# A Nystrom attention and two MLP layers on one core: how q and k are turned, when weights are narrowed, where block 2's weights are put

## The chip, the cores and the metric

One core of one Trainium2 chip runs the whole program in one launch. The metric is device time in microseconds (us); here the median of three runs of the kernel before. Engines are named as in the profile: PE (TensorE matmul), PEld (its weight loads), DVE (VectorE), ACT (ScalarE), POOL (GpSimd), SP (SyncE, which issues most DMAs).

## The reference

q, k, v are 4 batches x 8 heads x 576 rows x 64. Every 18 rows of q and k are averaged to 32 landmarks. Three softmaxes follow, A from q and the landmarks of k, B from both landmarks, C from the landmarks of q and k, and an iterated inverse of B:

```python
A, Bm, C = sm(q, k_lm), sm(q_lm, k_lm), sm(q_lm, k)
Z = Bm.T / (norm1(Bm) * norminf(Bm) + 1e-6)
for _ in range(6):
    Z = 2 * Z - Z @ Bm @ Z
x = (A @ Z @ C @ v)                          # 2304 tokens x 512
h = x @ w_in;  g = max(h, 0) + alpha * min(h, 0);  x = g @ w_out      # d_ff 2048
h = x @ w_in2; g = h * clip(h + 3, 0, 6) / 6;      out = g @ w_out2
```

The weights arrive as 64-bit floats and are narrowed to 32 bits on the core.

## The kernel before, in words

**Stages.** The attention of batch 0 runs alone at the start (`attention(0, ..., lat=0)`). Then the first MLP layer (block 1) runs over the four batches, each in two half batches of 288 tokens, and the attention of the next batch runs in between (`bg`, a background generator that is stepped by `tick`, three times per step). Last comes the second MLP layer (block 2) over five groups of 512 or 384 tokens.

**Steps.** A half batch has 16 steps, one for each 128 columns of the hidden layer (`NK` = 16). `items` is the list of all steps; `at_` is the step's number in its batch, 0 to 31 (L896). `Block1.first` (L741) forms h on PE and applies the activation on ACT and DVE. `Block1.second` (L767) multiplies by w_out into four accumulators `acc`, two steps later (`LOOK`, L733; three for the first one). Block 1 doesn't multiply x by w_in: `project` (L667) multiplies w_in by `bd`, the small product of the inverse, C and v of each head, so that A of the batch can be multiplied by the result. One call covers 512 columns, that is four steps, into two PSUM banks of a pool that has two (`two`, L226); its casts (`split`, L126) are ACT work and then DVE work, and free the banks.

**Narrowing.** A piece of 128 x 512 weights lands as pairs of 32-bit words (`landed`, L180). `words_of` (L189) is two ACT instructions on it (L196, L199), `joined` (L201) one DVE instruction (L206). `w_in_tiles` (L627) goes through w_in: the first 512 columns (block c = 0) as eight half pieces, the others as four pieces each; each of its steps issues the words of one piece and the join of the one before. Its loads of blocks 2 and 3 use the four buffers that block 0's pieces leave. `w_out_tiles` (L690) narrows one piece of w_out a step. The first half batch uses w_out in plain 32-bit; later ones use pairs of 32-bit parts made by `w_out_split` (L695).

**Order.** In `attention(0, ...)` all engines but POOL keep the order in which the code issues (`manual_schedule`, L708). In the main loop (L888) only PE and SP do; the order on ACT and DVE is set by a planner, by a modelled timeline and the order of issue. `behind(insts)` (L172) makes what it encloses follow the given instructions in the queue of the same engine; it adds no wait on another engine. In the first half batch, step `at_` issues narrowing up to a count, w_in up to piece `at_ + 12`, w_out up to `at_ + 3`, all behind `started`, the split of project(0,0)'s first 256 columns (L726). The second 256 columns and project(0,1) are issued at step 1. The last two query tiles of A (`rest`, L590) are in `bg` from step 0; batch 1's attention enters it at step 8 and is finished at step 28, ahead of project(1,0).

**The turns of q and k.** `transposed_long` (L282): a load has rows p x 4 + t on partition p. For each of the four head pairs eight matmuls with the identity (four t by two heads, each two instructions in the profile) write a PSUM bank in the order (t, p), ACT copies the bank to SBUF with a write of stride four words (L299), DVE sums over the landmarks (L300). `warm(n)` (L711) issues n matmuls on zeros to an idle bank.

**Block 2's weights.** 32 units (`units2`, L860), in the order `order2`: four tiles of w_in2, four of w_out2, for each of four chunks. Each is loaded to a place, narrowed and split there. `homes` lists the places: at first new ones and one spare, then those of block 1's projected w_in and of w_out, which come free as the last half batch uses them for the last time. Odd batches use the hidden columns in another order (`part`, L623): blocks 2, 3, 0, 1. `land2` issues loads, `upto2` narrowing, up to a count that grows with the step.

## Time and profile before

| what | value |
|---|---|
| median of 3 runs | 897.0 us (896.64 to 897.53) |
| profiled execution | 897.17 us, span 895.2 us |
| mean granted clock of TensorE | 0.979 |
| PE, PEld, DVE, ACT busy | 849.7, 726.8, 420.6, 381.7 us |
| L758 relu, 128 x 288, ACT | 410 ns each, x116 |
| L128 cast of gs, 128 x 288, ACT | 433 ns each, x112 |
| L206 join, 128 x 512, DVE | 691 ns each, x32 in block 2 |
| L430 scores of A, first half batch, PE wait ahead | 3.8 us |

The span runs from the first to the last instruction of the profiled execution; its own time is 2 us longer. A busy PE is not PE at its peak: `warm` matmuls count as busy. In the rows below a line begins with a start and a duration in us (timeline, chain of waits), or with the bounds of a stretch. In the timeline the duration reaches to the end of the last matmul of a group, so groups overlap by some 0.2 us; the chain of waits counts from one to the next. In brackets stands the time that the engine was idle before, and what released it. A clock of 1.00 is TensorE's full speed.

### The profile page before, as it was taken

The page shows a single profiled execution, that of the slowest core. Times are in us where ns is not written, and L with a number is a line of the kernel's source. Part 1 is how long each engine was busy: PE and PEld are TensorE (multiplying, and loading weights), DVE is VectorE, ACT ScalarE, POOL GpSimd, SP SyncE. Part 2 cuts the span into 40 slices and gives each one's busy share as a digit, 9 for nine tenths or more (in the row PEclk, how much of TensorE's full clock was granted, in tenths as well). Part 3 has the DMA queues.
Part 4 walks back from the last instruction along what each step waited for, and adds up shares of the span by engine and source line. Part 5 has one row for each costly group of instructions (what it writes and reads, how often), then busy time and mean ns, then how long its engine had stood idle before and what let it go on. Part 6 is the DMA issues. An engine that isn't in the chain of part 4 may idle for free.

```text
span 895.2 us, 13601 instructions
## 1 busy us (share of the span) xinstructions
PE 849.7 (95%) x5487; PEld 726.8 (81%) x5487; DVE 420.6 (47%) x880; ACT 381.7 (43%) x811; POOL 27.6 (3%) x51
## 2 busy tenths in 40 slices
PE   9856999999999999999999499999999999999997
PEld 4524779989999989988998388888888888989996
DVE  3677457755754557468447822232223222223222
ACT  4488245545434544358449922222222222222222
POOL 0000001010010101010100000000000000000000
PEclk9977999999999999999999799999999999999999
DMA  7986312351044311059227600210021002000000
GB/s 229 408 306 209 67 40 68 85 156 54 1 107 128 89 38 55 1 181 367 86 73 244 246 0 1 94 48 0 1 71 48 0 1 88 30 1 12 25 0 36
DMA packets 60847, 82.68 MB, mean 92 GB/s; under 512 B 35696, under 2 KB 43888, under 8 KB 59504
## 3 DMA queue, kind: packets, MB, share of 16 engines
q1 hardware_dynamic: 57648, 68.18, 24.0%
q0 software_dynamic: 3136, 13.63, 4.1%
q8 instruction: 43, 0.70, 0.3%
q14 instruction: 20, 0.16, 0.1%
HBM read 63.45 MB, written 18.35 MB: 91 GB/s over the span
## 4 chain that ended last, share of the span: by engine, by line
PE 82%; ACT 8%; DMA 5%; DVE 2%; issue 1%; SPq 1%; ACTq 0%; DVEq 0%
PE h L134 30%; PE oacc L134 22%; PE acc L134 17%; DMA raw<-in_moe_w_in_dram 3%; ACT raw L196 3%; ACT raw L199 3%; PE acc L776 3%; PE wp L676 2%; DMA raw<-in_moe_w_out_dram 2%; PE tp L271 1%; PE sa L430 1%; ACT w L128 1%; PE idle L713 1%; PE sc L343 1%; PE psr L514 1%
## 5 line engine op out<-in xcount | busy, mean ns | idle before, releaser
L134 PE MATMUL oacc<-w,g 128*128 128x512 f32 x864 | 211.5, 394 | 11.4 <-ACT g L128 11.4
L134 PE MATMUL acc<-gs,wout 128*128 128x288 f32 x1344 | 208.4, 300 | 4.4 <-DVE gs L129 2.4
L134 PE MATMUL h<-ysb,w 128*128 128x512 f32 (+1 forms) x960 | 210.5, 368 | 0.0
L134 PEld LDWEIGHTS oacc<-w,g 128*128 128x128 f32 x864 | 163.2, 190 | 44.7 <-ACT g L128 11.8
L134 PEld LDWEIGHTS h<-ysb,w 128*128 128x128 f32 x960 | 176.6, 188 | 25.0
L134 PEld LDWEIGHTS acc<-gs,wout 128*128 128x128 f32 x1344 | 185.2, 188 | 10.1 <-DVE gs L129 3.7
L807 DVE SCALAR_TENSOR_TENSOR t<-t,h 128x512 f32<-128x512 f32 (+1 forms) x80 | 50.8, 635 | 220.6 <-ACT t L806 220.6
L806 ACT ACTIVATE t<-h,three 128x512 f32<-128x512 f32 (+1 forms) x80 | 51.6, 645 | 218.9 <-PE h L134 218.7
L134 PE MATMUL h<-a,w 128*128 128x288 f32 x768 | 130.1, 306 | 3.1 <-DVE gs L755 2.6
L134 PEld LDWEIGHTS h<-a,w 128*128 128x128 f32 x768 | 109.8, 190 | 21.8 <-DVE gs L129 11.1
L758 ACT ACTIVATE t<-h 128x288 f32<-128x288 f32 x116 | 47.6, 410 | 70.4 <-PE h L134 69.7
L759 DVE SCALAR_TENSOR_TENSOR t<-t,beta,h 128x288 f32<-128x288 f32 x112 | 57.2, 511 | 43.2 <-ACT t L758 42.1
L129 DVE TENSOR_TENSOR g<-t,g 128x512 fp32r<-128x512 f32 (+1 forms) x80 | 51.1, 639 | 45.8 <-ACT g L128 45.5
L128 ACT CAST g<-t 128x512 fp32r<-128x512 f32 (+1 forms) x80 | 46.1, 578 | 51.2 <-DVE t L807 51.2
L128 ACT CAST gs<-t 128x288 fp32r<-128x288 f32 x112 | 48.5, 433 | 44.4 <-DVE t L759 44.1
L129 DVE TENSOR_TENSOR gs<-t,gs 128x288 fp32r<-128x288 f32 x112 | 50.9, 454 | 29.7 <-ACT gs L128 29.5
L196 ACT ACTIVATE raw<-raw 128x512 f32<-128x512 f32 (+1 forms) x68 | 44.6, 659 | 8.1 <-DMA raw<-in_moe_w_in_dram 6.1
L199 ACT ACTIVATE raw<-raw 128x512 int32<-128x512 uint32 (+1 forms) x68 | 43.8, 648 | 0.0
L776 PE MATMUL acc<-gs,raw 128*128 128x288 f32 x128 | 36.3, 421 | 0.0
L676 PE MATMUL wp<-win,bd 64*32 64x512 f32 (+1 forms) x272 | 21.4, 602 | 11.7 <-DVE w L129 9.5
L206 DVE SCALAR_TENSOR_TENSOR x<-raw 128x512 int32<-128x512 int32 x32 | 22.1, 691 | 15.2 <-ACT raw L199 14.9
L776 PEld LDWEIGHTS acc<-gs,raw 128*128 128x128 f32 x128 | 24.3, 202 | 5.6 <-issue 1.0
(170 smaller groups left out, 583.6 us busy)
## 6 DMA issues: line engine op xcount, KB each, us to landing
raw<-in_moe_w_in_dram SPq DMA_DIRECT2D x32, 512.0 KB, 7.2
raw<-in_moe_w_out_dram SPq DMA_DIRECT2D x32, 512.0 KB, 10.2
win<-w_in SPq DMA_DIRECT2D x6, 1024.0 KB, 4.8
ysb<-y_d SPq DMA_DIRECT2D x6, 1024.0 KB, 13.6
y_d<-ys POOLq DMA_DIRECT2D x16, 288.0 KB, 3.6
y_d<-a POOLq DMA_DIRECT2D x16, 288.0 KB, 4.0
out_dram<-ob SPq DMA_DIRECT2D x18, 256.0 KB, 2.0
rk<-in_k_dram SPq DMA_DIRECT2D x16, 256.0 KB, 4.8
```

What stands on the lines that cost most here:

```text
L128: nc.scalar.copy(hi, src),
L129: rest.tensor_tensor(out=lo, in0=src, in1=hi.bitcast(F32), op=ALU.subtract),
L134: nc.tensor.matmul(ps, lhsT=lhs(x), rhs=rhs(y), start=first and i == 0, stop=last and i == 2)
L196: nc.scalar.activation(out=high.bitcast(F32), in_=high.bitcast(F32), func=AF.Prelu, scale=2.0 ** -112, alpha=-(2.0 ** 32))
L199: nc.scalar.activation(out=low, in_=low.bitcast(U32), func=AF.Copy, scale=0.9374 * 2.0 ** -29)
L206: nc.vector.scalar_tensor_tensor(out=to.bitcast(I32), in0=high, scalar=3, in1=low, op0=ALU.logical_shift_left, op1=ALU.bitwise_or)
L676: nc.tensor.matmul(ps[g][js], lhsT=bd_t[b][gp, js], rhs=w[gp, j, cols], start=True, stop=True)
L758: nc.scalar.activation(out=t, in_=h, func=AF.Relu, scale=-1.0),
L759: nc.vector.scalar_tensor_tensor(out=gs[:, 0] if plain else t, in0=t, scalar=beta[:, kk:kk + 1], in1=h, op0=ALU.mult, op1=ALU.add),
L776: nc.tensor.matmul(acc, lhsT=words[kk][:, ms], rhs=gs[:, 0], start=at_ == 0, stop=at_ == NK - 1)
L806: nc.scalar.activation(out=t, in_=h, func=AF.Relu, bias=three, scale=1.0)
L807: nc.vector.scalar_tensor_tensor(out=t, in0=t, scalar=6.0, in1=h, op0=ALU.min, op1=ALU.mult)
```

## The change

- In `transposed_long` the matmuls write every fourth word of the bank (`t:FULL:NF`), so that it is in order, and ACT's copy is dense. The tails warm once instead of three times, the turns not at all.
- `norms` is no longer a generator. In batch 0's attention the groups' maxima and exponentials stand in a loop with blocks and norms after the first; the pieces of `a0`, `a1` are moved, warm counts are lower, and nine steps of `early` (w_in narrowing) are issued in place of five.
- project(0,0)'s second 256 columns are issued at step 0 and are `started`; project(0,1) to (0,3) come at steps 3, 7 and 11 instead of 1, 5 and 9. Narrowing in step `at_` is issued behind `started` for three steps and then behind steps `at_ - 2` and `at_ - 3`; w_out goes first, up to `at_ + 2`, w_in up to `at_ + 10`.
- In the first half batch even steps use DVE for the activation, odd ones ACT and DVE (before: DVE for the first 12).
- `rest` enters `bg` at step 6.
- Block 2 has ten new places instead of eight; the places of w_out are listed in the order in which the last batch uses w_out; the counts of `land2` and `upto2` follow.

```diff
--- before.py
+++ after.py
@@ -286,21 +286,20 @@
             for j in range(NP):
                 nc.tensor.transpose(ps[:, j, :TAIL], tail[:, NG * j:NG * j + NG, :], ident[:TAIL, :TAIL])
             nc.scalar.copy(xt[:, :, FULL:S], ps[:, :, :TAIL])
-            warm(3)
+            warm(1)
             yield True
             for j in range(NP):
-                ps = bank("tp").rearrange("q (t p) -> q t p", t=NF)
+                ps = bank("tp")
                 for t in range(NF):
                     for g in range(NG):
                         nc.tensor.matmul(
-                            ps[64 * g:64 * g + 64, t], lhsT=full[:, NG * j + g, t * D:(t + 1) * D], rhs=ident,
+                            ps[64 * g:64 * g + 64, t:FULL:NF], lhsT=full[:, NG * j + g, t * D:(t + 1) * D], rhs=ident,
                             start=True, stop=True,
                         )
-                nc.scalar.copy(xt[:, j, :FULL].rearrange("q (p t) -> q t p", t=NF), ps)
+                nc.scalar.copy(xt[:, j, :FULL], ps)
                 nc.vector.tensor_reduce(
                     out=lm[:, j], in_=xt[:, j, :S].rearrange("p (l r) -> p l r", r=W), op=ALU.add, axis=AX.X
                 )
-                warm(3)
                 yield True
 
         if not lat:
@@ -408,7 +407,6 @@
             nc.vector.tensor_scalar(out=cc, in0=cc, scalar1=1e-6, scalar2=None, op0=ALU.add)
             nc.vector.reciprocal(out=cc, in_=cc)
             nc.vector.tensor_scalar(out=cn, in0=cc, scalar1=-1.0, scalar2=None, op0=ALU.mult)
-            yield True
 
         def c_scale():
             nc.vector.tensor_tensor(out=rs[:, :, 0:1], in0=sm[:, :, 0:1], in1=sm[:, :, 2:3], op=ALU.add)
@@ -556,35 +554,31 @@
             most_b(range(NG))
             for g in range(NG):
                 exp_b(g)
-            most_c(0, 1)
-            most_c(0, 0)
-            bias_c(0)
-            blocks()
-            warm(6)
-            exp_c(0)
-            n_ = norms()
-            drain(n_)
-            most_c(1, 1)
-            most_c(1, 0)
-            bias_c(1)
-            exp_c(1)
+            for g in range(NG):
+                most_c(g, 1)
+                most_c(g, 0)
+                bias_c(g)
+                exp_c(g)
+                if g == 0:
+                    blocks()
+                    warm(4)
+                    norms()
+            drain(turned_c(0))
+            next(a0)
             c_scale()
+            next(a1)
+            drain(turned_c(1))
+            next(early)
             warm(4)
-            drain(turned_c(0))
-            next(a1)
-            next(a0)
-            warm(2)
-            drain(turned_c(1))
-            warm(2)
             drain(product())
             n0, n1 = normalised([0, 1]), normalised([2])
             next(early)
-            fill = [a0, early, a1, early, a1, n0, early, n0, n1, early, n1, turned([0, 1]), turned([2])]
-            for _ in inverse():
-                for _ in range(2):
+            fill = [early, a0, a1, early, early, a1, early, n0, early, n0, n1, early, n1, early, turned([0, 1]), turned([2])]
+            for i, _ in enumerate(inverse()):
+                for _ in range(3 if i < 3 else 2):
                     if fill:
                         next(fill.pop(0), None)
-                warm(5)
+                warm(4)
             for x in fill:
                 next(x, None)
             rest.append(in_order(scores([3]), scores([4]), normalised([3]), normalised([4]), turned([3]), turned([4])))
@@ -607,7 +601,8 @@
         for x in pieces:
             yield from scores(x)
             yield from wait(1)
-        yield from norms()
+        norms()
+        yield True
         yield from alternate(turned_c(0), turned_c(1))
         yield from wait(1)
         yield from product()
@@ -729,7 +724,7 @@
     ps_o = pool("ps_o", 4, space=PSUM)
     ps_h = pool("ps_h", 2, space=PSUM)
 
-    w2, ysb = {}, {}
+    w2, ysb, steps = {}, {}, []
     LOOK = 2
 
     class Block1:
@@ -748,11 +743,12 @@
             plain = self.b == self.blk == 0
             t = mm.tile([P, HS], F32, tag="t", name="t")
             gs = mm.tile([P, 2, HS], F32 if plain else F32R, tag="gs", name="gs", bufs=5)
-            if plain and at_ < 3 * NK // 4:
+            if plain and at_ % 2 == 0:
                 nc.vector.tensor_scalar(
                     out=t, in0=h, scalar1=0.0, scalar2=minus[:, kk:kk + 1], op0=ALU.min, op1=ALU.mult
                 )
-                nc.vector.tensor_tensor(out=gs[:, 0], in0=t, in1=h, op=ALU.add)
+                self.last = [nc.vector.tensor_tensor(out=gs[:, 0], in0=t, in1=h, op=ALU.add)]
+                steps.append(self.last)
                 return gs
             self.last = [
                 nc.scalar.activation(out=t, in_=h, func=AF.Relu, scale=-1.0),
@@ -760,6 +756,7 @@
                     out=gs[:, 0] if plain else t, in0=t, scalar=beta[:, kk:kk + 1], in1=h, op0=ALU.mult, op1=ALU.add
                 ),
             ]
+            steps.append(self.last)
             if not plain:
                 split(gs[:, 0], gs[:, 1], t)
             return gs
@@ -867,7 +864,7 @@
             yield True
 
     bg = Background()
-    emitted = [NP + 1, 0, 0]
+    emitted = [0, 2 * NP + 1, 0]
 
     def pinned(gen):
         while True:
@@ -876,7 +873,6 @@
                     return
             yield True
 
-    bg.add(pinned(rest[0]))
     g2, ring = [], [0]
     units = Background(units2())
     done2 = [0]
@@ -897,13 +893,13 @@
 
             if n < n1:
                 if b == 0 and at_ < NK:
-                    for i, (gen, upto) in enumerate(((w_gen, min(at_ + 12, NK + 5)), (wo_gen, min(at_ + 3, NK)))):
-                        with behind(started):
+                    if at_ == 0:
+                        started = project(0, 0, slice(256, 512))
+                    for i, (gen, upto) in enumerate(((wo_gen, min(at_ + 2, NK)), (w_gen, min(at_ + 10, NK + 5)))):
+                        with behind(started if at_ < 3 else steps[at_ - 2] + steps[at_ - 3]):
                             gen.step(upto - emitted[i])
                         emitted[i] = upto
-                    if at_ == 1:
-                        project(0, 0, slice(256, 512))
-                    if at_ % 4 == 1 and at_ // 4 + 1 < NC:
+                    if at_ % 4 == 3 and at_ // 4 + 1 < NC:
                         project(0, at_ // 4 + 1)
                 if b == 0 and at_ >= NK - 2:
                     upto = min(NK, at_ - NK + 3)
@@ -913,6 +909,8 @@
                 if b == 0 and at_ in (NK + 4, NK + 6):
                     c = NC // 2 + (at_ - NK - 4) // 2
                     nc.gpsimd.dma_start(out=keep[:, c], in_=wins[c])
+                if b == 0 and at_ == 6:
+                    bg.add(pinned(rest[0]))
                 if b == 0 and at_ == 8 or b and at_ == 5:
                     if b + 1 < B:
                         bg.add(rush(attention(b + 1, two, 1), 300))
@@ -927,17 +925,19 @@
                     stx.close()
                     wz = pool("wz", 1, side="right")
                     yp = pool("yp", 2, side="right")
-                    homes += [(wz, f"z{i}") for i in range(8)] + [(wa, f"s{NK - 1}")]
-                    free = [f"s{(i + NK) % (NK + 1)}" for i in range(NK)]
+                    nz = 10
+                    homes += [(wz, f"z{i}") for i in range(nz)] + [(wa, f"s{NK - 1}")]
+
+                    free = [f"s{(4 * part(b, i // 4) + i % 4 + NK) % (NK + 1)}" for i in range(NK)]
                     for i in range(NC):
                         homes += [(wc, f"c{2 * i}"), (wc, f"c{2 * i + 1}")] + [(wa, x_) for x_ in free[4 * i:4 * i + 4]]
-                    land2(9)
+                    land2(nz + 1)
                     load_y(0)
                     load_y(1)
                 if b == B - 1 and at_ > 4:
                     if at_ >= NK + 4:
-                        land2(min(len(order2), 9 + 6 * ((at_ - NK) // 4)))
-                    upto2(min(at_ - 4, 9) if at_ < NK + 4 else 9 + 5 * (at_ - NK - 3) // 4)
+                        land2(min(len(order2), nz + 1 + 6 * ((at_ - NK) // 4)))
+                    upto2(min(3 * (at_ - 3) // 4, nz + 1) if at_ < NK + 4 else nz + 1 + 5 * (at_ - NK - 3) // 4)
             if n == n1:
                 for _ in range(2):
                     pair = ay.tile([P, 2, 2, 512], F32R, tag="at", name="g2")
```

## Rows read from the trace of the kernel before

**Rows 1.** page, part 1: busy us of each engine, share of the span, instructions.
```profile
PE 849.7 (95%) x5487; PEld 726.8 (81%) x5487; DVE 420.6 (47%) x880; ACT 381.7 (43%) x811; POOL 27.6 (3%) x51
```

**Rows 2.** busy time by stretch: length, then busy us and count of each engine, clock, DMA, GB/s.
```profile
0.00:48.43 48.43, 44.37 (x405) 25.18 (x405) 23.38 (x73) 21.96 (x49) 1.52 (x9) 1.00 0.91 325
48.43:130.74 82.31, 62.81 (x381) 44.90 (x381) 51.58 (x104) 49.15 (x101) 2.87 (x6) 0.88 0.50 151
...
490.00:520.00 30.00, 18.63 (x70) 14.69 (x69) 21.52 (x34) 23.95 (x44) 2.63 (x4) 0.77 0.57 217
```

**Rows 3.** what PE waited for: us in total, times, longest us.
```profile
PE oacc L134 <- ACT g L128: 11.4, 1, 11.4
PE wp L676 <- DVE w L129: 9.5, 1, 9.5
```

**Rows 4.** chain of waits, the turns of k: start, us, what.
```profile
5.98 1.02 PE tp L295 x16
7.00 0.75 PE idle L713 x3
```

**Rows 5.** timeline of ACT, opening: start, us, what; behind it idle before and releaser.
```profile
20.64 1.08 ACT L299 COPY qT<-tp 128x512 f32<-128x512 f32 x1 [0.69 <-PE tp L295]
...
30.41 0.58 ACT L474 COPY ct<-ctp 128x512 f32<-128x512 f32 x1
...
41.77 0.21 ACT L530 COPY nx<-psr 128x64 f32<-128x64 f32 x1 [1.01 <-DVE nx L390]
```

**Rows 6.** timeline of DVE, opening.
```profile
21.75 0.75 DVE L300 TENSOR_REDUCE qlm<-qT 128x32 f32<-128x576 f32 x1 [1.01 <-ACT qT L299]
```

**Rows 7.** busy time by stretch, one us of the opening.
```profile
11.00:12.00 1.00, 1.00 (x16) 0.76 (x16) 0.27 (x1) 0.69 (x1) 0.00 (x0) 1.00 0.73 65
```

**Rows 8.** timeline of PE, first half batch.
```profile
48.43 0.79 PE L676 MATMUL wp<-win,bd 64*32 64x256 f32 x16
...
63.59 2.29 PE L676 MATMUL wp<-win,bd 64*32 64x512 f32 x16 [9.53 <-DVE w L129]
65.81 3.25 PE L134 MATMUL h<-a,w 128*128 128x288 f32 x12
...
77.51 5.35 PE L776 MATMUL acc<-gs,raw 128*128 128x288 f32 x16
```

**Rows 9.** chain of waits, first half batch.
```profile
93.72 1.94 PE acc L776 x8
95.66 0.80 PE h L134 x6
...
102.02 1.86 PE wp L676 x16
```

**Rows 10.** timeline of ACT, first half batch.
```profile
49.30 0.65 ACT L128 CAST w<-wp 128x256 fp32r<-128x256 f32 x2 [1.46 <-PE wp L676]
...
52.92 0.65 ACT L196 ACTIVATE raw<-raw 128x512 f32<-128x512 f32 x1
...
54.05 0.65 ACT L196 ACTIVATE raw<-raw 128x512 f32<-128x512 f32 x1
...
62.29 0.62 ACT L128 CAST w<-wp 128x256 fp32r<-128x256 f32 x2
```

**Rows 11.** chain of waits, start of block 2.
```profile
505.29 0.66 ACT raw L196
...
506.91 0.67 ACT raw L196
...
510.82 5.49 PE oacc L134 x12
...
519.41 2.72 PE oacc L134 x12
```

**Rows 12.** timeline of PE, second half batch: end of the next batch's attention.
```profile
169.35 0.44 PE L537 MATMUL psv<-r,vd 128*64 128x128 f32 x4
...
173.91 1.09 PE L676 MATMUL wp<-win,bd 64*32 64x512 f32 x16
```

## The prediction

> **What bounds the kernel now.** I read the page's part 1 first: TensorE (PE) is busy 95% of the span [rows 1], so only the stretches in which it stands still, or works for nothing, can be shortened. The busy times by stretch find them [rows 2]. Opening, 0 to 48.43 us: PE looks busy (44.37), but `warm` matmuls are part of that; the chain of waits shows each turn of a head pair as 1.02 us of transposes and 0.75 of warm, one after the other [rows 4]. First half batch, 48.43 to 130.74: PE stands 82.31 - 62.81 = 19.5 us, at a mean clock of 0.88 instead of 1.00. Start of block 2, 490 to 520: 11.4 us idle. Elsewhere PE is the bound. The table of PE's waits has the two long ones [rows 3]: 11.4 us for ACT's cast `g` (L128) and 9.5 us for DVE's split `w`.
>
> Their cause is order on ACT. At 49.83 ACT begins to narrow weights and does nothing else until 62.29, where the casts of the second half of project(0,0) come [rows 10], 12 us late; project(0,1) needs their PSUM banks and waits until 63.59 [rows 8]. At 494 to 510 the same happens to `g`: weight units of 506.91 - 505.29 = 1.62 us each lie ahead of it, and PE resumes at 510.82 [rows 11].
>
> **1. The turns of q and k.** Eight turns lose warm(3), two tails go from 3 to 1. Before the last turn that is 7 x 0.75 + 2 x 0.5 = 6.25 us less [rows 4]; the eighth warm lay beside ACT and DVE. Behind the last turn stand the copy and the reduction, 1.08 and 0.75 us [rows 5, 6]. The copy's write becomes dense; a dense 512-column copy from PSUM took 0.58 [rows 5]: 0.5 less. Together 6.75. What is late next: per turn PE 1.02, DVE 0.75, ACT 0.58, so PE still sets the pace. Data: the traffic falls to 65 GB/s in the twelfth us [rows 7], so k and q are in by about 12; the last turn would begin at about 13.3. SP issues v when k's buffer is free, at about 9.5 instead of 12.4, with the weight loads behind it, also earlier.
>
> The price is PE's write of every fourth word of a bank. No row has such a write. Floor: 0 (it can't beat a dense write). Ceiling from the nearest strided write, ACT's of the same 16-byte stride into SBUF: 1.08 against 0.58, a factor of 1.86 [rows 5]; 0.86 x 1.02 x 8 = 7.0 us. I take 0: in a turn 16 matmuls of 128 columns take 1.02 us, two at a time on separate partitions, so a partition receives a word per 1.0 ns, while a warm matmul of 512 columns takes 0.25 us, a word per 0.5 ns [rows 4]. The write has half of its shown rate to spare.
>
> The Trainium skill speaks against this (PSUM — Partial Sum Buffer, Specifications (TRN2)): lines of 8 bytes, and any access pattern that isn't contiguous slows matmuls significantly. It gives no factor; by it this part would keep less than its 6.75 us. No run here shows it.
>
> **2. From scores to product.** VectorE's order is as before: first group's maximum, blocks, norms, second group's maximum. So "C v ahead of the norms" buys nothing by itself. warm 6 to 4 ahead of the norms' matmul saves about 0.4, since that matmul began when the warm ended; warm(4) behind the last turn of C, in place of 2 + 2, costs about 0.4 ahead of the product. Moving the reduction of `a0` ahead of c_scale is hidden, as c_scale is used only after the product. Sum 0.
>
> **3. Narrowing in the inverse.** Nine steps of w_in in place of five: 4 x 2 ACT activates on half or whole pieces and 4 DVE joins, about 3 and 1.5 us of work. Cover: ACT stands about 1 us in each iteration (as 1.01 ahead of 41.77) [rows 5]. On the chain it is between 0 and 4.5; I take 0.5, near the floor since the idle times are as long as a piece. warm 5 to 4 ahead of psv and ahead of the projection saves 2 x 0.2. Sum 0.
>
> Opening: -6.7, bounds -6.75 + 7.0 + 4.5 = +4.8 and -7.2.
>
> **4. First half batch.** What can be won is the 19.5 us idle plus the slow clock: project 2.29 against 1.86, six-matmul `h` 1.6 against 0.8 twice, sixteen `acc` 5.35 against 3.88 [rows 8, 9], about 3.2 after taking off 0.2 per group for the drawn-out end of its last matmul: 22.7. What stays (times on the old clock, before part 1 is taken off):
> - project(0,0)'s second half now stands before h(0) and needs the banks of the first: ACT's casts, 0.65 [rows 10], and DVE's split behind them: 1.3 idle.
> - Narrowing is queued behind that second half's casts, so ACT starts it at 51.85. project(0,1) needs the last piece of block 1. Ahead of it, in order of issue, stand w_out 0 to 3 and three pieces of w_in; a piece takes 54.05 - 52.92 = 1.13 us [rows 10]; seven and one relu make 8.2: 60.0, the join 60.7. PE has h(0) to h(2) until 54.2: 6.5 idle.
> - The clock falls in that gap; after the 11.4 us gap at 510.82 the slow restart cost 5.49 - 2.72 plus 0.4 [rows 11]: 3.1.
> - About 1 of small waits.
>
> That is 11.9; the gain is 22.7 - 11.9 = 10.8. From 60.7 on PE has 2.74 us per step (h 0.80, acc 1.94 [rows 9]) and a projection every fourth: 3.2. ACT has two pieces (2.25), half a relu and a quarter of two casts: 2.7, so it keeps up; even steps on DVE, odd on ACT, divide the rest. A piece of w_out issued at step n is used by PE at step n+3, and the gate is step n-2, so the gate has five steps of cover; were it gone, the lockstep below. The loads of blocks 2 and 3 move from step 1 to 3 in the program, but SP has nothing between, and they start when their buffers are released, as before. Bounds: the wait at project(0,1) gone with its clock, -20.4; the same wait once more at project(0,2), -1.2.
>
> **5. The remaining tiles of A** move from step 0 to 6. They leave the start-up, but the next batch's attention begins two steps later. Its psv came at 169.35, two steps ahead of project(1,0) at 173.91 [rows 12]; now they meet. PE waits for one copy there: 0 to 1.5, I take 0.7.
>
> **6. Block 2.** In the last half batch, w_out tiles 8 to 15 are used first, so listing their places first frees the first of them eight steps earlier, some 19 us at 2.4 a step (psv and project(1,0) are 4.56 apart, a little under two steps [rows 12]). Two more places need no release: eleven units instead of nine are done before. Left for the first steps of block 2: six units, not eight, and loads that are not late. The gain is at most 11.4 plus the slow restart 3.1 = 14.5. Steps 20 to 31 now issue 15 units: ACT 15 x 1.62 + 12 x 0.65 (relu and cast of the table ahead, each overlapping the next by 0.1) = 32.1 us for PE's 28.8, 3.3 over; I let that much be lost: -11.2. Bounds: 0 (the cast still behind the units) and -14.5.
>
> Sum: -6.7 - 10.8 + 0.7 - 11.2 = -28.0. The profiled execution took 897.17 (span 895.2), the median of the runs is 897.0: both give 869.
>
> **Rivals.**
> - No wait at project(0,1): -9.6 more, 860. For: PE idles only by ACT's order there. Against: four w_out pieces are issued ahead of what the projection needs.
> - The strided write costs its ceiling: +7.0, 876. For: ACT's factor. Against: PE's write rate.
> - `g` is still behind weight units: +11.2, 880. For: nothing ties units to steps there. Against: loads land earlier.
> - Slower: lockstep. Narrowing behind step n-2 and the step behind narrowing become a loop: h 0.8, relu 0.4, two pieces 2.25, join 0.7 (relu and join by the table ahead), acc 1.94, and a quarter of projection, casts and split (4.2) make 7.1 a step, 16 x 7.1 = 114 against 82.3: +32 there, 897 + 32 - 6.7 - 11.2 = 911. It decides from (82.3 + 17.9)/16 = 6.3 us a step. Against: five steps of cover.
> - The turns do nothing because data come late: last q landing at 18 rather than 12 would give back 5: 874; rows 7 speak against it.
>
> **Chances.** Forecast 869 (861 to 878) 0.50; no wait 860, 0.15; strided 876, 0.12; `g` 880, 0.12; late data 0.03; lockstep 911, 0.06; no change 0.02. The range takes in everything but the lockstep and the far tails of the bounds: 852 to 885. 0.2% (1.8 us) is about what can be told from no change. Faster 0.91, same 0.02, slower 0.07.
>
> **What would show it.** Chain: eight turns of 1.02 us without warm between them, `sc` resuming near 15.8 instead of 22.5; if the turns are 1.9, the strided write is paid. PE: a gap of 5 to 7 us ahead of the first full-width project, then none above 1 us until the seventeenth `h`, near 113 instead of 130.74. Clock near 1.00 after that gap. ACT: pieces between relus, not in one block. Around block 2: no PE wait above 4 us, `g` within 2 us of its DVE input. Wrong: PE waits in every step of the first half batch, or units waiting for DMA in the last one.

## The result, and the profile after

The changed kernel takes 872.1 us (median of four runs, 870.9 to 873.1) where the kernel before took 896.9 (896.6 to 897.5): a ratio of 0.972, 95% interval 0.9705 to 0.9738. 869 (852 to 885) was forecast. The profiled execution took 870.9, the fastest of the four and 26.3 less than the one of before: its span is 869.0, 26.2 less, and 1.9 lie around it (2.0 before).

Part 1 of the page after, for [rows 1]:
```profile
PE 837.6 (96%) x5446; PEld 720.8 (83%) x5446; DVE 416.2 (48%) x876; ACT 377.5 (43%) x815; POOL 27.7 (3%) x51
```
TensorE still has 31 us in which it stands. To see where the 26.2 us came from, cut both spans at the same four pieces of work: project(0,0), project(1,0), a point 202 us behind that (TensorE stands for 0.4 us between the two in either kernel), and the first `h` of block 2. The first stretch of before, 48.43 us, stands in [rows 2]; the busy times by stretch of the others (columns as in [rows 2]; PE, PEld, DVE, ACT, POOL, then granted clock):
```profile
48.43:173.91 125.48, 105.52 (x760) 84.63 (x759) 85.25 (x192) 73.89 (x163) 5.63 (x10) 0.92 0.41 118
173.91:376.00 202.09, 201.72 (x1745) 184.08 (x1745) 120.41 (x290) 93.10 (x238) 12.22 (x20) 1.00 0.27 75
376.00:477.08 101.08, 96.69 (x735) 90.40 (x734) 58.31 (x116) 59.31 (x132) 5.50 (x8) 1.00 0.51 176
477.08:895.20 418.12, 401.44 (x1850) 342.48 (x1848) 133.23 (x212) 133.43 (x230) 2.76 (x4) 0.98 0.13 46
```
and the same stretches after:
```profile
0.00:42.01 42.01, 34.94 (x365) 22.17 (x365) 24.61 (x76) 21.09 (x57) 2.23 (x10) 1.00 0.95 329
42.01:154.01 112.00, 104.07 (x760) 83.27 (x759) 81.82 (x187) 71.59 (x159) 4.95 (x9) 0.98 0.50 150
154.01:356.00 201.99, 201.62 (x1744) 184.01 (x1745) 119.79 (x288) 93.22 (x238) 12.25 (x20) 1.00 0.27 75
356.00:465.37 109.37, 98.67 (x736) 90.74 (x735) 73.26 (x142) 80.41 (x174) 5.51 (x8) 1.00 0.63 223
465.37:869.00 403.63, 398.29 (x1850) 340.63 (x1848) 116.76 (x188) 111.22 (x187) 2.77 (x4) 1.00 0.09 31
```
Read down the first column: -6.4, -13.5, -0.1, **+8.3**, -14.5; together -26.2. Three stretches won and one lost. In the fourth, PE's matmuls are the same, ACT's busy time has grown from 59 to 80 us, and PE stands 10.7 us instead of 4.4.

**The opening.** PE's timeline after, the turns of k and of q, then the first two rows of scores:
```profile
5.49 3.97 PE L295 MATMUL tp<-ident,rk 128*64 128x128 f32 x64
...
10.10 3.71 PE L295 MATMUL tp<-ident,rq 128*64 128x128 f32 x64
13.74 1.39 PE L342 MATMUL sc<-kT,qlm 64*32 64x320 f32 x6
15.29 1.24 PE L342 MATMUL sc<-kT,qlm 64*32 64x320 f32 x26 [0.15 <-DVE qlm L300]
```
and from ACT's timeline one copy, where [rows 5] had 1.08:
```profile
12.99 0.59 ACT L299 COPY qT<-tp 128x512 f32<-128x512 f32 x1 [0.29 <-PE tp L295]
```
Four turns in a row take 3.71 to 3.97 us, 0.93 to 0.99 each, with nothing between; [rows 4] had 1.02 and then 0.75 of warm. The strided write costs PE nothing that can be seen (e1_dense below is the test), and ACT's dense copy costs 0.59. The bulk of `sc` resumes at 15.29 (forecast 15.8, before 22.55).

**First half batch.** PE's timeline after, where [rows 8] had a 9.53 us gap:
```profile
43.75 0.99 PE L671 MATMUL wp<-win,bd 64*32 64x256 f32 x16 [0.96 <-DVE w L129]
44.67 1.84 PE L134 MATMUL h<-a,w 128*128 128x288 f32 x12
48.12 1.02 PE L134 MATMUL h<-a,w 128*128 128x288 f32 x6 [1.60 <-DVE gs L750]
49.07 1.60 PE L671 MATMUL wp<-win,bd 64*32 64x512 f32 x8
51.86 1.05 PE L671 MATMUL wp<-win,bd 64*32 64x512 f32 x4 [1.20 <-DVE win L206]
55.16 1.05 PE L671 MATMUL wp<-win,bd 64*32 64x512 f32 x4 [2.25 <-DVE win L206]
56.14 1.81 PE L134 MATMUL h<-a,w 128*128 128x288 f32 x6
57.75 4.94 PE L773 MATMUL acc<-gs,raw 128*128 128x288 f32 x16
```
Four short gaps, 6.0 us in all, where one long one stood. project(0,1) does twelve of its sixteen matmuls between the pieces of w_in that it waits for. ACT's timeline of the same time says why it waits at all:
```profile
45.35 0.69 ACT L196 ACTIVATE raw<-raw 128x512 f32<-128x512 f32 x1
...
53.21 0.38 ACT L754 ACTIVATE t<-h 128x288 f32<-128x288 f32 x1
...
58.00 1.04 ACT L128 CAST w<-wp 128x512 fp32r<-128x512 f32 x2
```
From 45.35 on, narrowing runs without a break (seven pieces) until the relu of step 1, four more follow, and the casts of project(0,1) come at 58.00: the order that [rows 10] showed, on a smaller scale. The clock falls for a moment; stretches of the same time (the last three columns are granted clock, DMA, GB/s):
```profile
56.00:58.00 2.00, 2.00 (x9) 1.86 (x8) 1.26 (x2) 2.00 (x4) 0.00 (x0) 0.54 0.83 340
58.00:60.00 2.00, 2.00 (x6) 1.43 (x6) 1.41 (x3) 2.00 (x6) 0.00 (x0) 0.61 0.94 266
60.00:62.00 2.00, 2.00 (x10) 1.63 (x9) 1.51 (x3) 2.00 (x4) 0.00 (x0) 1.00 0.57 199
```

**Last half batch and block 2.** The table of PE's waits after (us, times, longest); both rows of [rows 3] are gone, and these lead:
```profile
PE acc L134 <- ACT gs L128: 7.2, 6, 2.2
PE wp L671 <- DVE win L206: 3.5, 2, 2.3
PE acc L134 <- DVE gs L129: 3.4, 9, 0.5
```
Before, the first and the third were 2.0 and 2.4. Two lines of ACT's timeline show how the loss begins:
```profile
426.27 0.67 ACT L196 ACTIVATE raw<-raw 128x512 f32<-128x512 f32 x1 [3.08 <-DMA raw<-in_moe_w_in_dram]
...
430.58 0.67 ACT L196 ACTIVATE raw<-raw 128x512 f32<-128x512 f32 x1 [2.79 <-DMA raw<-in_moe_w_out_dram]
```
and PE's timeline where it ends:
```profile
432.67 0.40 PE L134 MATMUL acc<-gs,wout 128*128 128x288 f32 x1 [2.18 <-ACT gs L128]
```
A weight unit of block 2 stands at the head of ACT's queue and waits for its load; the casts of `gs` that PE needs stand behind it. The other five waits for `gs`, of 0.26 to 1.56 us, come otherwise; the longest in PE's timeline:
```profile
459.61 0.40 PE L134 MATMUL acc<-gs,wout 128*128 128x288 f32 x1 [1.56 <-ACT gs L128]
```
From 433 to 461, where three of them fall, ACT is busy 27.9 of 28.0 us: the casts stand behind pieces of weights whose loads have landed. At the start of block 2, where [rows 11] had 5.49 us behind an 11.4 us gap, PE now goes straight on:
```profile
484.86 2.88 PE L134 MATMUL h<-ysb,w 128*128 128x512 f32 x12
487.58 2.88 PE L134 MATMUL oacc<-w,g 128*128 128x512 f32 x12
```

### The profile page after: what moved, and what is told of

It is laid out like the page before. It is cut to its first block, busy times and chain, and to the rows that moved or that the text cites. A ratio compares the mean times of both kernels' runs of the same rounds, so it can differ in the third digit from the quotient of the medians.

```text
span 869.0 us, 13515 instructions
## 1 busy us (share of the span) xinstructions
PE 837.6 (96%) x5446; PEld 720.8 (83%) x5446; DVE 416.2 (48%) x876; ACT 377.5 (43%) x815; POOL 27.7 (3%) x51
## 4 chain that ended last, share of the span: by engine, by line
PE 87%; ACT 6%; DMA 3%; DVE 2%; issue 1%; SPq 0%; ACTq 0%; DVEq 0%
PE h L134 33%; PE oacc L134 23%; PE acc L134 17%; PE acc L773 4%; DMA raw<-in_moe_w_out_dram 3%; PE wp L671 2%; PE sa L428 2%; ACT raw L199 2%; ACT raw L196 2%; PE tp L271 2%; ACT w L128 1%; PE sc L342 1%; PE idle L708 1%; PE tp L295 1%; PE pu L487 1%
## 5 line engine op out<-in xcount | busy, mean ns | idle before, releaser
L134 PE MATMUL acc<-gs,wout 128*128 128x288 f32 x1344 | 210.1, 301 | 10.7 <-ACT gs L128 7.2
L134 PE MATMUL oacc<-w,g 128*128 128x512 f32 x864 | 208.9, 390 | 0.0
L134 PEld LDWEIGHTS h<-a,w 128*128 128x128 f32 x768 | 108.9, 189 | 19.1 <-DVE gs L129 10.7
L129 DVE TENSOR_TENSOR gs<-t,gs 128x288 fp32r<-128x288 f32 x112 | 50.8, 454 | 26.7 <-ACT gs L128 26.5
L773 PEld LDWEIGHTS acc<-gs,raw 128*128 128x128 f32 x128 | 24.2, 201 | 5.4 <-issue 1.0
L129 DVE TENSOR_TENSOR w<-wp,w 128x512 fp32r<-128x512 f32 (+1 forms) x34 | 20.8, 655 | 16.1 <-ACT w L128 15.9
L206 DVE SCALAR_TENSOR_TENSOR x<-raw 128x512 int32<-128x512 int32 x32 | 22.1, 689 | 11.0 <-ACT raw L199 10.7
## 6 DMA issues: line engine op xcount, KB each, us to landing
raw<-in_moe_w_out_dram SPq DMA_DIRECT2D x32, 512.0 KB, 10.1
```

Of the source, the lines that this page charges most:

```text
L129: rest.tensor_tensor(out=lo, in0=src, in1=hi.bitcast(F32), op=ALU.subtract),
L134: nc.tensor.matmul(ps, lhsT=lhs(x), rhs=rhs(y), start=first and i == 0, stop=last and i == 2)
L206: nc.vector.scalar_tensor_tensor(out=to.bitcast(I32), in0=high, scalar=3, in1=low, op0=ALU.logical_shift_left, op1=ALU.bitwise_or)
L773: nc.tensor.matmul(acc, lhsT=words[kk][:, ms], rhs=gs[:, 0], start=at_ == 0, stop=at_ == NK - 1)
```

## The experiments

Times are medians; each kernel was timed beside the kernel before (897.3 to 897.7) on one chip. A profiled execution of one kernel differs from its other runs by up to 4.4 us, so stretches are compared as well as times.

**The parts alone.** Do the three gains and the loss belong to the parts they were put down to?

p1_turns: the kernel before with the turns alone changed.
```diff
-                ps = bank("tp").rearrange("q (t p) -> q t p", t=NF)
+                ps = bank("tp")
...
-                            ps[64 * g:64 * g + 64, t], lhsT=...
+                            ps[64 * g:64 * g + 64, t:FULL:NF], lhsT=...
...
-                warm(3)
```


> The kernel before with the turns of q and k alone changed (strided write, dense copy, warm 3 to 1 at the tails and 0 in the turns). Theory, the parts add up: the opening ends some 6.5 us earlier (project(0,0) near 42 instead of 48.43), every later stretch is only moved, about 890.5 us. Rival, the gain is swallowed: the weights' landing or ACT's block of narrowing holds the first half batch where it was, 895 to 897.


Measured 892.2 (ratio 0.994, 0.9927 to 0.9956): -5.2. Both rows of [rows 3] are still there (11.9 and 9.6).

p2_first: the changed kernel with the old turns and the old block 2, so with the edits of C, the inverse and the first half batch alone.
```diff
-                    free = [f"s{(4 * part(b, i // 4) + i % 4 + NK) % (NK + 1)}" for i in range(NK)]
+                    free = [f"s{(i + NK) % (NK + 1)}" for i in range(NK)]
...
-                    nz = 10
+                    nz = 8
```


> The changed kernel with the turns and block 2 as they were before, so that only the attention's reordering and the first half batch are changed. Theory, the parts add up: project(0,0) within 1 us of before, 13.5 us less between project(0,0) and project(1,0), about 883.5 us. Rival, the first half batch gains only because the opening brings the loads forward too: 5 us or less, 892 or more.


Measured 885.4 (0.986, 0.9847 to 0.9876): -12.0. project(0,0) to project(1,0) as in the changed kernel, and the last half batch as before, in its stretches:
```profile
50.05:161.95 111.90, 103.95 (x759) 83.03 (x759) 81.85 (x187) 71.44 (x159) 4.94 (x9) 0.98 0.45 130
161.95:465.05 303.10, 298.41 (x2476) 274.47 (x2477) 178.02 (x404) 152.40 (x370) 17.72 (x28) 1.00 0.35 108
```
The turns and their warm are the old ones too. So the first half batch's gain doesn't come from the shorter opening, and it isn't what costs the last half batch its time.

p3_block2: the kernel before with the places, the two more units and their counts alone.
```diff
-                    homes += [(wz, f"z{i}") for i in range(8)] + [(wa, f"s{NK - 1}")]
-                    free = [f"s{(i + NK) % (NK + 1)}" for i in range(NK)]
+                    homes += [(wz, f"z{i}") for i in range(10)] + [(wa, f"s{NK - 1}")]
+                    free = [f"s{(4 * part(b, i // 4) + i % 4 + NK) % (NK + 1)}" for i in range(NK)]
...
-                    upto2(min(at_ - 4, 9) if at_ < NK + 4 else 9 + 5 * (at_ - NK - 3) // 4)
+                    upto2(min(3 * (at_ - 3) // 4, 11) if at_ < NK + 4 else 11 + 5 * (at_ - NK - 3) // 4)
```


> The kernel before with block 2's places and unit counts alone changed. Theory: the last half batch grows by about 8 us, since ACT has more units there than it can take, and the start of block 2 loses its gap and slow restart of 14.5 us: 6.3 us less, about 890.7 us. Rival, the 8 us come from somewhere else (an earlier start that collides with other loads): then the last half batch stays as before and 14.5 us are gained, 882.5.


Measured 890.4 (0.992, 0.9901 to 0.9934): -7.0. PE's waits show both sides of it: `g` is gone, and the one on `gs` has come:
```profile
PE wp L676 <- DVE w L129: 10.0, 1, 10.0
PE acc L134 <- ACT gs L128: 5.7, 5, 1.6
```
project(1,0) to the first `h` of block 2 takes 310.8 us here, 303.2 before: +7.6, and block 2 gives back 14.5. The three sum to -24.2 where the whole gave -24.9: the parts add up, and the +8.3 belongs to this one.

**The strided write.** e1_dense: the changed kernel with PE's dense write and ACT's strided copy of before.
```diff
-                            ps[64 * g:64 * g + 64, t:FULL:NF], lhsT=...
+                            ps[64 * g:64 * g + 64, t], lhsT=...
...
-                nc.scalar.copy(xt[:, j, :FULL], ps)
+                nc.scalar.copy(xt[:, j, :FULL].rearrange("q (p t) -> q t p", t=NF), ps)
```


> The changed kernel with the turns' write dense again and ACT's copy strided, without warm. Theory, the strided PSUM write is free and the copy's stride is what costs: PE's 16 matmuls take the same 0.93 to 1.02 us, ACT's 1.08 us copy sets the pace, 8 x 0.13 + 0.5 = 1.6 us more, about 873.7 us. Rival, the strided write costs PE something that its early data hide: turns get shorter than 0.93 us and the time is 871 or less.


Measured 874.2 (0.974, 0.9722 to 0.9758), near the 873.7 of the theory. PE's timeline, the turns of q:
```profile
10.55 3.71 PE L295 MATMUL tp<-ident,rq 128*64 128x128 f32 x64
```
and ACT's copies of q as a group (busy us and mean ns, then idle before them):
```profile
L299 ACT COPY qT<-tp 128x512 f32<-128x512 f32 x4 | 3.9, 1144 | 0.4 <-PE tp L295 0.4
```
64 matmuls in 3.71 us, to the hundredth what the strided write takes above; the copies take 1.1 us each where dense ones take 0.59. In these rows the stride of 16 bytes is free on PE's way into PSUM and costs ACT nearly its own time on the way into SBUF. By the Trainium skill (PSUM — Partial Sum Buffer, Specifications (TRN2)) the strided write should have been slower; this row doesn't agree, and the measurement decides for this shape (f32, 128 columns, matmuls that write the two halves of the partitions in turn).

**The tie.** e3_not_tied: narrowing behind project(0,0)'s second half only, free of the steps.
```diff
-                        with behind(started if at_ < 3 else steps[at_ - 2] + steps[at_ - 3]):
+                        with behind(started):
```


> The changed kernel with all narrowing of the first half batch behind project(0,0)'s split only, as before, at the changed counts and places of the projections. Theory, the tie to the steps does the work: ACT runs ahead with narrowing, the casts of project(0,1) and the relus wait behind it again, and the first half batch gives back 5 to 13 us: 877 to 885. Rival, where project(0,0) and project(0,1) stand does the work, and the tie nothing: 871 to 873.


Measured 878.5 (0.980, 0.9782 to 0.9818), +6.4 on the changed kernel. Two of PE's lines that the changed kernel doesn't have:
```profile
63.82 0.53 PE L134 MATMUL h<-a,w 128*128 128x288 f32 x2 [1.39 <-ACT w L128]
...
81.23 0.97 PE L428 MATMUL sa<-bdk,qT 128*64 128x64 f32 x8 [3.04 <-DVE w L129]
```
Casts stand behind pieces that have run ahead, well past the start. The stretch grows from 112.0 to 118.4: the tie is worth 6.4 of the 13.5 us; the other 7.1 come with the rest of the edits of parts 4 and 5, which no run took apart.

**Places in order of release.** e4_old_places: the changed kernel with the places in index order again (the `free` line of p2_first).


> The changed kernel with block 2's reused places in the order of their index again, ten new places and the counts as changed. Theory, the order of release matters: loads wait for the place of w_out 0 until about 450, units jam ahead of the cast g, PE waits about 11 us there and restarts slowly, while the last half batch loses its 8 us of waits: 876 to 880. Rival, two more places and the higher count are enough: 871 to 873.


Measured 877.6 (0.978, 0.9766 to 0.9796), +5.5. PE's timeline has the gap of [rows 11] again:
```profile
493.45 4.39 PE L134 MATMUL oacc<-w,g 128*128 128x512 f32 x12 [10.06 <-ACT g L128]
```
and the stretch ahead takes 306.9 instead of 311.4: late releases hold back the units in the last half batch, and they meet `g` instead. So the order of release removes that gap, and moves a part of its cost into the last half batch.

**What costs the 8.3 us?** The first theory was that too many units were issued there. e5_units_later issues 17 instead of 26 ahead of block 2:
```diff
-                    upto2(... else nz + 1 + 5 * (at_ - NK - 3) // 4)
+                    upto2(... else nz + 1 + 7 * (at_ - NK - 3) // 13)
...
-                    upto2(min(len(order2), 24 + 2 * (r + 1)))
+                    upto2(min(len(order2), 18 + 2 * (r + 1)))
```


> The changed kernel with 17 units issued by the end of the last half batch instead of 26, then two per step of block 2. Theory, the 8 us of waits in the last half batch are ACT oversubscribed by units, and units that wait for their loads at the head of ACT's queue; six units less per twelve steps leave ACT idle time: 5 us less, about 867 us, with no long wait in block 2. Rival, the units then jam ahead of g in block 2, whose gap comes back: 875 or more.


Measured 873.2 (0.973, 0.9718 to 0.9749): nothing. PE waits 7.5 us for `gs` instead of 7.2, and ACT runs 29 pieces of these units before block 2 in both. The planner sets ACT's order, and issuing the units later in the program didn't place them later. So this run failed as a test of the number of units.

e8_units_tied makes each unit follow the casts of the step before it, one a step:
```diff
+                casts.append(split(gs[:, 0], gs[:, 1], t))
...
-                    upto2(min(3 * (at_ - 3) // 4, nz + 1) if at_ < NK + 4 else nz + 1 + 5 * (at_ - NK - 3) // 4)
+                    with behind(casts[-1]):
+                        upto2(min(3 * (at_ - 3) // 4, nz + 1) if at_ < NK + 6 else nz + 1 + at_ - NK - 5)
...
-                    upto2(min(len(order2), 24 + 2 * (r + 1)))
+                    with behind(casts[-1]):
+                        upto2(min(len(order2), 21 + 2 * (r + 1)))
```


> The changed kernel with block 2's units in the last batch and in block 2's first steps issued behind the casts of the step before, from step 22 of the batch on one per step, then two. Theory, a unit count alone doesn't hold the planner, which puts units on ACT as soon as their loads are modelled to be there; PE's waits of 10.6 us for gs come from casts queued behind such units and behind loads that haven't landed. Tied, most of them go: the stretch from project(1,0) to the first h of block 2 shrinks from 311 to about 304 us, 865 us in all. Rival, it is ACT's total work: the waits stay, or come back as a gap in block 2, 871 or more.


Measured 858.7 (0.956, 0.9541 to 0.9582): 13.3 better than the changed kernel, more than expected. The stretch from project(1,0) to block 2:
```profile
158.12:454.19 296.07, 295.70 (x2477) 273.99 (x2477) 185.57 (x417) 161.55 (x390) 17.76 (x28) 1.00 0.41 132
```
and ACT's pieces as a group (busy, mean ns, idle time before them and what ended it):
```profile
L196 ACT ACTIVATE raw<-raw 128x512 f32<-128x512 f32 (+1 forms) x68 | 44.8, 659 | 0.0
```
The same line of the changed kernel:
```profile
L196 ACT ACTIVATE raw<-raw 128x512 f32<-128x512 f32 (+1 forms) x68 | 44.0, 648 | 7.6 <-DMA raw<-in_moe_w_out_dram 4.5 <-DMA raw<-in_moe_w_in_dram 3.1
```
PE stands 0.4 us in 296, and no unit waits for its load any more. That takes away more than the change had added: the kernel before had waits of this kind too (303.2 us for this stretch). The tie did two things at once: 21 pieces now run before block 2 instead of 29, and those that run do not wait at the head of the queue. e5 was to separate the two and didn't; the next run and e4 do it, below.

e11_tied_old_places: the tied units, with the places in index order.


> The run with tied units, with the reused places in the order of their index again. Theory, the tie orders ACT's queue but a unit at its head still waits for its load: loads for the place of w_out 0 can't start before about 440, so PE's waits for gs return: 863 to 870. Rival, the order of release was only needed because units weren't tied: 857 to 860.


Measured 866.9 (0.965, 0.9634 to 0.9668), 8.2 worse than e8: within the expectation, but not by the wait expected. The last half batch stays free (0.9 us for `gs`), and `g` waits again. PE's timeline:
```profile
483.16 4.81 PE L134 MATMUL oacc<-w,g 128*128 128x512 f32 x12 [5.18 <-ACT g L128]
```
and ACT's:
```profile
482.49 0.62 ACT L128 CAST g<-t 128x512 fp32r<-128x512 f32 x1 [2.29 <-DMA y_d<-a]
```
This cast stands behind units until 480.20, and then 2.29 us longer, until a store of `a` to `y_d` has landed, as `g` takes the buffers of `a` (both have the tag `at`). In the changed kernel a cast of `g` waits 1.90 us for that store too, and PE waits for nothing there. The two stores of `a` take 8.0 us (median) from issue to landing here, the second is issued at 475.8, and 415 to 420 GB/s are moved from 474 to 482; in e8, whose weight loads are done by then, they take 2.9. Late places make late loads; that these delay the store, which nobody had on the list, is inferred from this one pair of runs.

Was it the number of units or their order? ACT's pieces of weights in the stretch ahead of block 2, in the kernel before and then in the changed one (busy us and mean ns, then idle before them and what ended it):
```profile
L196 ACT ACTIVATE raw<-raw 128x512 f32<-128x512 f32 x15 | 10.3, 687 | 8.0 <-DMA raw<-in_moe_w_in_dram 6.1 <-DMA raw<-in_moe_w_out_dram 1.8
...
L196 ACT ACTIVATE raw<-raw 128x512 f32<-128x512 f32 x29 | 19.8, 681 | 6.4 <-DMA raw<-in_moe_w_out_dram 3.3 <-DMA raw<-in_moe_w_in_dram 3.1
```
The waits for loads were there before the change, and were longer. What the change added is 14 pieces. The same count for the other runs:

| kernel | pieces on ACT ahead of block 2 | their waits for loads, us | project(1,0) to block 2, us |
|---|---|---|---|
| before | 15 | 8.0 | 303.2 |
| changed | 29 | 6.4 | 311.4 |
| e5_units_later | 29 | 8.2 | 313.4 |
| e4_old_places | 17 | 9.8 | 306.9 |
| e11_tied_old_places | 17 | 2.1 | 297.5 |
| e8_units_tied | 21 | 0.0 | 296.1 |

e4 and e11 have equally many pieces and the same places: there the tie, with its own counts, is worth 9.3 us. From the changed kernel to e4, both without a tie, 12 pieces fewer are worth 4.5, though the waits for loads are longer. So both count, and the 8.3 us that the change added go with the number of pieces, not with the waits for loads.

**The wait at project(0,1).** e6_w_first puts the pieces that it needs ahead of w_out's.
```diff
-                    for i, (gen, upto) in enumerate(((wo_gen, min(at_ + 2, NK)), (w_gen, min(at_ + 10, NK + 5)))):
+                    for i, gen, upto in ((1, w_gen, min(max(at_ + 10, 13), NK + 5)), (0, wo_gen, min(at_ + 2, NK))):
```


> The changed kernel with w_in's pieces of block 1 issued ahead of w_out's in step 0. Theory, project(0,1) waits only because w_out pieces stand ahead on ACT: its two waits of 3.5 us go, about 868.7 us. Rival, the wait moves on to the first acc, which needs w_out 0 and 1, now later on ACT: 871 to 873.


Measured 872.3 (0.972, 0.9700 to 0.9742): no change, a miss. The projection runs through, and the next `h` waits:
```profile
56.73 1.06 PE L134 MATMUL h<-a,w 128*128 128x288 f32 x6 [3.95 <-DVE gs L755]
```
It needs a PSUM bank that step 1's activation frees, and its relu stands on ACT behind the pieces.

e9_w_first_dve puts that activation on DVE as well, and narrowing behind the casts.
```diff
-            if plain and at_ % 2 == 0:
+            if plain and (at_ % 2 == 0 or at_ == 1):
...
-                        with behind(started if at_ < 3 else steps[at_ - 2] + steps[at_ - 3]):
+                        with behind(started if at_ < 3 else steps[at_ - 2] + steps[at_ - 3] + list(started)):
```


> The changed kernel with w_in's pieces of block 1 first in step 0 and step 1's activation on DVE instead of ACT. Theory, in the run with w_in first alone the wait only moved to h(3), which needs the bank of h(1), whose relu stood behind the narrowing on ACT (3.9 us); with that relu off ACT both waits go: 868.5 us. Rival, the next thing on ACT, the casts of project(0,1), is late by as much: 871 to 873.


Measured 871.8 (0.972, 0.9704 to 0.9733): a miss again. The wait is now one step on, at the casts of project(0,1):
```profile
60.40 0.53 PE L134 MATMUL h<-a,w 128*128 128x288 f32 x2 [2.39 <-ACT w L128]
```
e10_both takes e8's tied units, w_in first, step 1 on DVE, holds w_out at two pieces until step 3, and issues project(0,1) ahead of step 3's narrowing, so that its casts come before it:
```diff
+                    if at_ == 3:
+                        started = project(0, 1)
```


> The run with tied units, and in the first half batch: w_in's pieces of block 1 first, step 1's activation on DVE, and project(0,1) issued ahead of step 3's narrowing, which goes behind its casts; w_out only up to two pieces until then. Theory, each earlier attempt moved the wait to the next thing behind narrowing on ACT; now bank, relu and casts are all ahead of it, and 2.4 to 3.5 us go: about 855.5 us. Rival, another wait follows (w_out 2 late for the third acc): 857 to 860, as with tied units alone.


Measured 856.6 (0.954, 0.9530 to 0.9556). It is the fastest version, 40.9 us below the kernel before. Against e8 the median is 2.2 lower, but the intervals overlap (e8's ends at 0.9541), and the two traces differ by 1.2 us already at project(0,0), ahead of any edit; from project(0,0) to project(1,0) e10 takes 111.2 us for 112.9. A wait is left, one step further:
```profile
63.06 1.06 PE L134 MATMUL h<-a,w 128*128 128x288 f32 x6 [2.32 <-DVE gs L755]
```
Three ways of removing it moved it; in each, the next thing that PE needs stands on ACT behind narrowing. What was gained is at the edge of what can be told.

## Why the prediction came out

869 was forecast and 872.1 measured. The three mechanisms were there, but two terms were mis-sized by some 3 and 5 us in opposite directions, so that the total came this near is in part luck.

- **Parts 1 to 3, the opening: right for the turns, 0.8 to 3.8 us short behind them.** Forecast -6.7, profiled -6.4. The value of 0 for the strided write was right (e1_dense: 3.71 us either way), and the rival at 876 is dead; the working for it (a word per 1.0 ns of a shown 0.5) is not tested, as no run wrote faster. p1_turns reaches project(0,0) 6.9 us earlier than the kernel before, as worked out; its profile gives 0.9 back in the first half batch and 0.6 in block 2, which leaves -5.4 (-5.2 in medians). Parts 2 and 3, put at 0, cost 0.8: from where `sc` resumes to project(0,0) it takes 25.9 us in the kernel before and in p1_turns, 26.7 in p2_first and in the changed kernel. And that is the good case. Seven of the nine profiled executions with this opening lose another 1.5 to 3.0 us in it: their granted clock from 22 to 29 us is 0.70 to 0.76, where the changed kernel's own profile and e4's have 1.00. The same warm matmuls in the changed kernel and then in e8:
```profile
23.70 1.03 PE L708 MATMUL idle<-idle 128*128 128x512 bf16 x4
...
24.35 1.91 PE L708 MATMUL idle<-idle 128*128 128x512 bf16 x4
```
So -6.4 is what an execution without this slow spell shows; most have one, and the forecast had no term for it.
- **Parts 4 and 5: right in kind, 3.4 too small.** Forecast -10.8 + 0.7 = -10.1, profiled -13.5. The step that failed is "PE has h(0) to h(2) until 54.2: 6.5 idle". Its end was right (project(0,1) is through 14.1 us after project(0,0) began, as worked out), but it took the projection as one block behind the last piece, while twelve of sixteen matmuls ran between pieces. Waits of 0.96 + 1.60 + 3.45 = 6.0 stand in place of 1.3 + 6.5 = 7.8; the 1.60 at h(2), for a PSUM bank held by the activation of step 0, was not listed. "The clock falls in that gap" was right, with 3.1 too much: `h` 1.81 and acc 4.94 against 0.80 and 3.88, less 0.2 each, is 1.7. The seventeenth `h` came at 107.8, not 113; a part of that is the attention work that part 5 moves behind it. The projection of the second half batch waits 0.38 and psv 0.18: 0.6 for the 0.7 taken. The lockstep never came: e3 shows that the tie earns 6.4.
- **Part 6: right gain, wrong price.** The whole ceiling of 14.5 was won at block 2. "3.3 over; I let that much be lost" failed: the loss was 8.3. The term that failed is the 15 units of steps 20 to 31: that is what the program issues there, and ACT ran 18 (424.74, where step 20 begins, to 465.37). By the same sum 18 are 37.0 us for PE's 28.8, 8.2 over. The waits for loads, 6.4 us there, were in no term; but the kernel before has 8.0 of them and lost less. I had written this sign down as what would prove me wrong (units waiting for DMA in the last half batch), and it came; as it stood in the kernel before too, it could prove little. The forecast held because the first half batch gave 3.4 more. The order was a chance that the forecast didn't see: with units tied, and 8 fewer ahead of block 2, this stretch is 15.3 us shorter (e8).

The rivals: no wait at project(0,1) (860) did not come by this change, and e6, e9 and e10 show that the wait moves when it is pushed. `g` still behind units (880) is what e4 makes (877.6). Late data: `sc` resumed at 15.29, so no.

## What to carry to other kernels

Cost background work on an in-order engine by the pieces that will run ahead of what the bound engine needs, not by those that the program issues by then: here a planner ran 29 for 26, and 29 for 17. A piece that may wait for a transfer belongs behind the casts that the bound engine needs next, by a tie in the program, as its place in the issue order alone can change nothing. When a long wait is a projection or cast on pieces that arrive one by one, count what can run between the pieces. After removing a wait, look for its cost upstream: here places for weights that came free earlier put 29 pieces on ACT ahead of block 2 where 15 had stood. And where a gain hangs on the granted clock, read it from more than one execution.

## What was not expected of the hardware

- PE writing f32 into PSUM with a stride of 16 bytes: 64 matmuls of 128 columns in 3.71 us, the same as dense. ACT writing SBUF with that stride: 1.1 us against 0.59 for 128x512.
- In the changed kernel waits of 1.60, 1.20 and 2.25 us between 46.5 and 55.2 were followed by 4 us at a granted clock of 0.54 to 0.61; in e10_both a single 2.32 us wait at 61 us was followed by eight acc in 2.10 us, as fast as their neighbours, and in e9_w_first_dve one of 2.39 and 0.33 by eight in 3.27. In the opening one and the same wait, 1.84 us for `epc` ahead of the transposes of C, was followed by a clock of 1.00 in two executions and by a slow spell in seven, with the same instructions; why isn't shown. p1_turns and p2_first, which each keep one half of the old opening, had none in one profile each; there that wait is 0.62 us or doesn't occur.
- The store of `a`, 288 KB, lands 2.9 us (median) after its issue in e8 beside a quiet DMA, and 8.0 in e11 beside 415 to 420 GB/s; ACT's 2.29 us of waiting for it is a part of PE's 5.18.
